# Attention rows by halves of the head: values, key sums and division in column tiles of 32, weights rounded in pieces of 768

## Chip, core and metric

One core of one Trainium2 chip. The metric is device time in microseconds (us) from the first to the last instruction of an execution, with what lies around it; lower is better. All times are of single executions, or medians over several.

The engines: PE multiplies matrices (a matmul has a stationary operand, loaded ahead, and a moving one; the trace lists the loads as PEld), DVE and POOL work on tensors element by element, ACT applies functions and copies, and SP issues the DMAs here, in the order of the program. On chip, a tensor has up to 128 partitions and a row of elements in each. PE writes into eight banks of an accumulator memory (PSUM).

## What is computed

```python
def rmsnorm(x, g):
    return x / np.sqrt(np.mean(x * x, axis=-1, keepdims=True) + 1e-06) * g

# q, k, v: (8, 12, 448, 64); w_in: (768, 2048); w_out: (2048, 768)
q_n, k_n = rmsnorm(q, g_q), rmsnorm(k, g_k)
scores = 1.0 / np.sqrt(64) * np.matmul(q_n, k_n.transpose(0, 1, 3, 2))
attn = np.exp(scores - np.max(scores, axis=-1, keepdims=True))
attn = attn / (np.sum(attn, axis=-1, keepdims=True) + 1e-09)
x = np.matmul(attn, v).transpose(0, 2, 1, 3).reshape(8 * 448, 768)
h = x @ w_in
out = (h - np.tanh(h)) @ w_out
```

The two weights arrive as float64, as pairs of 32-bit words, and are rounded to float32 on the chip. All else is float32.

## The kernel before

**Steps.** Attention is cut into 48 steps: 8 batches by 6 pairs of heads. A step s loads k, q and v of two heads (`load`), takes the mean squares of rows (`norm`: POOL squares into `sq`, L325; DVE sums, L326; POOL raises to the power -0.5, L330), scales q (`norm_q`, L336), turns k and q on PE (`turn`, L348 and L352), multiplies keys by queries (`scores`, L372; row tiles of 64), and takes exponentials on ACT (L377), with no maximum subtracted, as the gains bound the scores. So keys lie in the partitions of `p`, in four chunks of 112, and queries in its rows.

**Sums and values.** `values` (L398) multiplies v by `p`: for each chunk and head a matmul with 64 stationary columns and 448 moving ones; head 0 fills partitions 0 to 63 of a bank, head 1 the other 64. The sum over keys is a matmul with ones. From step 8 on, `add` (L389, L391) first adds the four chunks on DVE, so that one part is left for PE; the steps before have four. `totals` (L410) uses 64 columns of ones, so the sums come out repeated over the partitions as the values lie, and `divide` (L452) multiplies by their reciprocal (L415) in one instruction; its output is scattered with a step of four elements, since a chunk takes every fourth row. Steps 12 to 47 use `totals_by_halves` (L425): four column tiles of 32, each with one head and one half of the queries; the reciprocal has 224 elements in a row then (L430), but does not lie as the values do. So one row of each tile goes to DRAM (`rows_out`, L435) and comes back repeated over 64 partitions (`rows_in`, L443).

**MLP.** After a batch's six steps its x, 6 tiles of 128 x 448, goes through both products by a scheme with seven products in place of eight, on halves of rows and columns. `divide` makes the sums of tiles that it needs for steps 3 to 5 of a batch (`tt`, L465 to L468, on DVE in batch 0, on POOL later). `hidden` makes 28 products for a batch, 12 matmul records each, and evicts each from its bank in `use` (L562 to L583); `project` makes 21 (L620 to L634); batch 0 uses `project_first` (L659) with plain products. All run as a stream of matmuls that the slots advance by a planned number of nanoseconds (`run`).

**Slots.** Instructions of each engine run in the order of the program, which is written out by hand. `first_slot` runs for s from -3 to 5: no MLP yet. `slot` runs for steps 6 to 11, with batch 0's MLP between, `late_slot` for steps 12 to 47. In a `first_slot` the order is: `scores` of step s+1 (first half), `turn` of s+2, loads of s+4, `norm` of s+3, weights, `totals` of s, `scores` (second half), `divide(values)` of s, `norm_q` of s+3, weights. PSUM banks go round: 5 for scores and the like, 3 for products.

**Weights.** Rounding a piece takes two ACT instructions (L71, L72), three on DVE (L78, L79, L82) and one on POOL (L90). Before, there are 64 pieces of 128 x 384. `weight(to)` goes on to piece `to`: it issues part a of a piece, part b of the one before, part c of finished ones, and loads for as many further pieces as have room: the first 16 in nine places of the later tensor gT, then four buffers `w_raw`. `due` says at which product which piece must be done. After 8 pieces `combine_weights` (L260 to L263) makes the sums of blocks for the seven products, and `keep_weights` stores them in DRAM; `combine_w_out` (L278 to L283) does so for w_out. Batches 1 to 7 read them back through a ring of six places (`ring_load`, L311 and L313).

Of the kernel before, what the change touches and what calls it, by code (L numbers as in the profile page):

```python
# [20 lines left out]
NCH = 4  # L21
# [71 lines left out]
def bounded_path(tc, ctx, q, k, v, moe_w_in, moe_w_out, out, g_col, ident, ones, neg_half):  # L93
# [14 lines left out]

    nc = tc.nc
# [11 lines left out]
    EARLY = 16  # L121
# [60 lines left out]
    NSTAGE = CF * S // DM  # L182
# [10 lines left out]
    def weight_piece(n):  # L193

        if n < 2 * CF:
            j, f, blk = n // 8, n % 8 // 4, n % 4
            p, low, i = ((1, 0, 0), (0, 1, 0), (4, 1, 1), (2, 0, 1))[blk]
            return 2 * j + f + low * HF, i, built(j, p)[:, f]
        i, f = 1 - (n - 2 * CF) // CF, n % CF
        if i == 0:  # L200
            f = f // 2 + f % 2 * HF
        return f, i, w_out_row(f, i)

    def weight_load(n):

        f, i, _ = weight_piece(n)
        if n < EARLY:
            raw = stage[:, n % NSTAGE * DM : (n % NSTAGE + 1) * DM].rearrange("p (f w) -> p f w", w=2)
        else:
            raw = wp.tile([P, HALF, 2], I32, name="w_raw", bufs=4)  # L210
        if n < 2 * CF:
            rows = w_in_words[i * HALF : (i + 1) * HALF, f * 2 * P : (f + 1) * 2 * P]
            nc.sync.dma_start(
                out=raw.rearrange("p (c f) w -> p c (f w)", c=HC),
                in_=rows.rearrange("(c p) f -> p c f", p=P),
            )
        else:
            nc.sync.dma_start(
                out=raw.rearrange("p f w -> p (f w)"),
                in_=w_out_words[f * P : (f + 1) * P, 2 * i * HALF : 2 * (i + 1) * HALF],  # L220
            )
        raws[n] = raw
# [4 lines left out]
    def place_free(n):  # L227

        if n < EARLY:
            return n - NSTAGE < done[2]  # L230
        return n - 4 < max(done[2], EARLY)

    def weight(to):

        while done[1] < min(to, 4 * CF):
            n = done[1]
            round_weight_a(nc, raws[n], weight_piece(n)[2])
            if n:
                round_weight_b(nc, raws[n - 1], weight_piece(n - 1)[2])
            done[1] = n + 1  # L240
            finish_weights(n - 1 if n < EARLY else n)
            while done[0] < min(n + 6, 4 * CF) and place_free(done[0]):
                weight_load(done[0])
                done[0] += 1
            if kept[1] < kept[0] and n >= 8 * kept[0] + 3:
                keep_weights()
        if done[1] == 4 * CF > done[2]:
            round_weight_b(nc, raws[4 * CF - 1], weight_piece(4 * CF - 1)[2])
            finish_weights(4 * CF)

    def finish_weights(to):
        while done[2] < to:
            round_weight_c(nc, raws.pop(done[2]), weight_piece(done[2])[2])
            done[2] += 1
            if done[2] % 8 == 0 and done[2] <= 2 * CF:
                combine_weights(done[2] // 8 - 1)
# [136 lines left out]
    def values(s, av):  # L393
        v_nat = loaded.pop(("v", s))
        for c in range(NCH):
            p = probs[s, c // 2]
            for h in range(2):
                nc.tensor.matmul(  # L398
                    av[h * D : (h + 1) * D, :S], lhsT=v_nat[:, h, c, :], rhs=p[:, h, c % 2, :],
                    start=(c == 0), stop=(c == NCH - 1),  # L400
                )
        return av

    def totals(s, dn):

        t = sums.pop(s)
        parts = t if t else [probs[s, c // 2][:, :, c % 2, :] for c in range(NCH)]
        for i, p in enumerate(parts):
            for h in range(2):
                nc.tensor.matmul(  # L410
                    dn[h * D : (h + 1) * D, :S], lhsT=ones[:CP, :D], rhs=p[:, h, :],
                    start=(i == 0), stop=(i == len(parts) - 1),
                )
        rd = whole[s] = sp.tile([P, S], F32, name="rd")
        nc.vector.reciprocal(rd, dn[:, :S])  # L415

    def totals_by_halves(s, dn):

        t = sums.pop(s)
        parts = t if t else [probs[s, c // 2][:, :, c % 2, :] for c in range(NCH)]  # L420
        for i, p in enumerate(parts):
            for h in range(2):
                for n in range(2):
                    r = (2 * h + n) * BL
# [7 lines left out]
    def rows_out(s):  # L432
        rs = whole[s]
        row = whole[s] = scratch.tile([2, S], F32, name="row", bufs=2)
        nc.sync.dma_start(  # L435
            out=row.rearrange("h (n q) -> (h n) q", n=2), in_=rs.rearrange("(g i) q -> g i q", i=BL)[:, 0, :]
        )

    def rows_in(s):

        row = whole[s]
        rd = whole[s] = sp.tile([P, S], F32, name="rd")
        nc.sync.dma_start(  # L443
            out=rd,
            in_=bass.AP(tensor=row.tensor, offset=row.offset, ap=[[S, 2], [0, D], [1, S]]),
        )

    def divide(s, av):
        b, hp = steps[s]
        rd = whole.pop(s)  # L450
        x = xT[b, hp] = xp.tile([P, S], F32, name="xT")
        nc.vector.tensor_tensor(  # L452
            out=x.rearrange("r (p c) -> r c p", c=NCH), in0=av[:, :S].rearrange("r (c p) -> r c p", c=NCH),
            in1=rd.rearrange("r (c p) -> r c p", c=NCH), op=ALU.mult,
        )
# [17 lines left out]

    due = [min(EARLY + m + 1, 3 * 8) for m in range(9)]
    due += [3 * 8 + m + 1 for m in range(8)]
    due += [2 * CF + CF * (m + 1) // 11 for m in range(11)]
    assert len(due) == 7 * SETS and due[-1] == 3 * CF
# [7 lines left out]
    def products(b, layer, count, width, depth, moving, done_with):  # L485
# [8 lines left out]
        def product(j, p, bank, first):  # L494
            if b == 0:
                weight(due[7 * j + ORDER.index(p)])
                w = built(j, p).rearrange("p f (c d) -> p (f c) d", d=P)
# [3 lines left out]
            for f in range(width):  # L501
                for c in range(depth):
                    nc.tensor.matmul(  # L503
                        bank[:, f * HS : (f + 1) * HS], lhsT=w[:, f * depth + c, :], rhs=moving[p](c),
# [19 lines left out]
    def hidden(b):  # L524
# [17 lines left out]
        def done_with(j):  # L542
            up, down = slice(2 * j, 2 * j + 2), slice(HF + 2 * j, HF + 2 * j + 2)
            s1, s2, s5, u3 = part("s1"), part("s2"), part("s5"), part("u3")
# [14 lines left out]
            def use(p, bank):  # L559
# [9 lines left out]
                elif p == 7:  # L569
                    nc.vector.tensor_tensor(out=u3, in0=v, in1=s5, op=ALU.add)  # L570
                    nc.vector.tensor_tensor(out=s1, in0=v, in1=s1, op=ALU.add)

                    def rest():
                        shrink(down, high, u3, nc.gpsimd)
# [31 lines left out]
    def project(b):  # L606
# [7 lines left out]
        def done_with(j):  # L614
            y1, y2, s1, s5 = (part(n).rearrange("p f s -> p (f s)") for n in ("s2", "u3", "s1", "s5"))

            def use(p, bank):
# [3 lines left out]
                elif p == 5:  # L621
                    nc.vector.tensor_tensor(out=s5[:, low], in0=v, in1=s1[:, low], op=ALU.add)
# [4 lines left out]
                elif p == 7:  # L627
                    nc.vector.tensor_tensor(out=y2[:, high], in0=v, in1=s5[:, low], op=ALU.add)
# [12 lines left out]
    def project_first(b):  # L641
# [6 lines left out]
        for m in range(CD * CF):  # L648
# [4 lines left out]
            if k < HC:  # L653
                weight(3 * CF + CF * (m + 1) // (HC * CF))
# [48 lines left out]
    def first_slot(s):  # L703
# [8 lines left out]
        ahead = 3 * (s + 4) if s < 0 else 9 + (EARLY - 9) * (s + 1) // NP  # L712
        weight(ahead - 2)
# [4 lines left out]
        weight(ahead - 1)  # L718
# [33 lines left out]
    def late_slot(s):  # L752
        gap = gap_ns(s)
        totals_by_halves(s, sc_bank())
# [5 lines left out]
        rows_out(s)  # L760
# [3 lines left out]
        rows_in(s)  # L764
# [15 lines left out]
    for n in range(4):  # L780
        weight_load(n)
    done[0] = 4
# [235 lines left out]
def kernel(  # L1018
# [45 lines left out]
    ones = consts.tile([P, D], F32, name="ones")  # L1064
# [41 lines left out]
```

## Time and profile before

| | |
|---|---|
| median of 6 runs | 1549.32 us (1548.81 to 1550.89) |
| profiled execution, its own time | 1549.49 us |
| its span, first to last instruction | 1547.4 us |
| PE busy | 1472.9 us (95%) |
| PE weight loads | 1158.8 us (75%) |
| DVE busy | 784.8 us (51%) |
| ACT busy | 425.7 us (28%) |
| POOL busy | 619.2 us (40%) |
| mean granted PE clock | 0.982 |
| DMA | 255.2 MB, mean 165 GB/s |
| HBM | 220.6 MB read, 33.2 MB written |

In the profile L398 is line 398 of the kernel; `out<-in` gives the tiles that an instruction writes and reads, then partitions x elements of each. "Busy" is time in which an engine executes; weight loads overlap the matmuls. A number behind `<-` is idle time of the engine, with the instruction that ended it. One f32 matmul appears as two MATMUL records. The granted clock is the share of full clock that PE was given.

### The profile page before, as it was taken

How to read it: one execution, taken by the hardware profiler on the slowest of the kernel's cores; microseconds unless marked ns; L12 is line 12 of the kernel's file. 1: busy time of each engine (PE TensorE's matmuls, PEld its weight loads, DVE VectorE, ACT ScalarE, POOL GpSimd, SP SyncE). 2: the span in 40 equal slices, each digit the busy share in tenths (PEclk: the TensorE clock that was granted, in tenths of full speed). 3: DMA queues.
4: the chain of work that ended last, by engine and by line, in shares of the span. 5: the costliest groups of instructions: out<-in, count | busy, mean ns of one | idle time of the engine just before them, and what ended most of it. 6: DMA issues, size and time to landing. Idle time of an engine off the chain costs nothing.

```text
span 1547.4 us, 20449 instructions
## 1 busy us (share of the span) xinstructions
PE 1472.9 (95%) x7584; PEld 1158.8 (75%) x7584; DVE 784.8 (51%) x1110; ACT 425.7 (28%) x817; POOL 619.2 (40%) x463
## 2 busy tenths in 40 slices
PE   3999879988999999999999999999999999999997
PEld 1347654437878878878888887887887888889997
DVE  6778888864543355435544445434553454432321
ACT  4463334412221232212322222222231222210100
POOL 6655555633442333523453244432453335311310
PEclk9999989998999999999999999999999999999999
DMA  7535554496546555465555554556546555456563
GB/s 192 161 96 165 171 179 135 136 283 200 162 161 171 154 173 168 142 182 164 155 186 152 156 172 153 172 159 168 168 154 177 151 170 165 135 153 179 181 201 95
DMA packets 255049, 255.22 MB, mean 165 GB/s; under 512 B 143308, under 2 KB 203356, under 8 KB 254940
## 3 DMA queue, kind: packets, MB, share of 16 engines
q1 hardware_dynamic: 254616, 253.81, 55.2%
q8 instruction: 63, 1.03, 0.3%
q14 instruction: 46, 0.38, 0.1%
q10 hardware_dynamic: 324, 0.00, 0.0%
HBM read 220.60 MB, written 33.16 MB: 164 GB/s over the span
## 4 chain that ended last, share of the span: by engine, by line
PE 77%; DVE 13%; POOL 3%; issue 2%; DMA 2%; SPq 2%; ACT 0%; ACTq 0%; DVEq 0%; POOLq 0%
PE mm L503 56%; PE sc L372 8%; PE sc L398 8%; DVE w_out L79 2%; POOL sq L325 2%; DVE rr L326 1%; DVE w_out L82 1%; DVE rd L415 1%; POOL rr L330 1%; PE sc L425 1%; PE mm L410 1%; DVE w_out L78 1%; PE mm L398 1%; PE sc L352 1%; PE sc L348 1%
## 5 line engine op out<-in xcount | busy, mean ns | idle before, releaser
L377 ACT ACTIVATE p<-sc,rr 112x448 f32<-112x448 f32 x384 | 212.5, 638 | 487.4 <-PE sc L372 406.2
L503 PE MATMUL mm<-xT,w_f 128*128 128x224 f32 x1392 | 284.4, 359 | 14.0 <-DMA w_f<-w_in 11.0
L503 PEld LDWEIGHTS mm<-xT,w_f 128*128 128x128 f32 x1392 | 264.4, 193 | 32.7 <-issue 25.7
L503 PEld LDWEIGHTS mm<-gT,w_f 128*128 128x128 f32 x1344 | 251.3, 190 | 23.7 <-issue 14.0
L503 PE MATMUL mm<-gT,w_f 128*128 128x224 f32 x1344 | 267.8, 355 | 0.0
L503 PE MATMUL mm<-tt,w_f 128*128 128x224 f32 x1044 | 213.1, 354 | 5.3 <-DVE s L583 3.5
L503 PEld LDWEIGHTS mm<-tt,w_f 128*128 128x128 f32 x1044 | 195.6, 190 | 15.7 <-issue 8.0
L503 PE MATMUL mm<-tg,w_f 128*128 128x224 f32 x1008 | 200.4, 353 | 0.0
L503 PEld LDWEIGHTS mm<-tg,w_f 128*128 128x128 f32 x1008 | 189.5, 190 | 0.0
L372 PE MATMUL sc<-qT,kT 64*112 64x448 f32 x768 | 177.9, 568 | 11.8 <-DVE rd L415 11.2
L540 POOL TENSOR_TENSOR gT<-s,th 128x448 f32<-128x448 f32 x64 | 77.7, 1214 | 238.5 <-ACT th L539 238.5
L330 POOL TENSOR_TENSOR rr<-rr,neg_half 112x16 f32<-112x16 f32 (+1 forms) x49 | 140.0, 2857 | 51.0 <-DVE rr L329 50.0
L325 POOL TENSOR_TENSOR sq<-q_nat 112x512 f32<-112x512 f32 x48 | 50.0, 1041 | 255.5 <-DVE rr L326 247.4
L372 PEld LDWEIGHTS sc<-qT,kT 64*112 64x112 f32 x768 | 63.8, 175 | 106.3 <-issue 80.5
L398 PE MATMUL sc<-p,v_nat 112*64 112x448 f32 x672 | 135.2, 544 | 0.0
L326 DVE TENSOR_REDUCE rr<-sq 112x8 f32<-112x512 f32 x96 | 64.9, 676 | 84.0 <-POOL sq L325 83.8
L391 DVE TENSOR_TENSOR sum<-sum,p 112x896 f32<-112x896 f32 x80 | 97.5, 1219 | 13.4 <-ACT p L377 8.6
L452 DVE TENSOR_TENSOR xT<-sc,rd 128x448 f32<-128x448 f32 x42 | 40.7, 969 | 124.1 <-PE sc L398 118.5
L466 POOL TENSOR_TENSOR tt<-xT,tt 128x224 f32<-128x224 f32 x21 | 24.7, 1176 | 187.4 <-DVE xT L452 187.4
L398 PEld LDWEIGHTS sc<-p,v_nat 112*64 112x64 f32 x672 | 45.0, 136 | 71.3 <-issue 69.4
L659 PE MATMUL mm<-gT,w_out 128*128 128x448 f32 x192 | 77.1, 555 | 0.4 <-POOL w_out L90 0.4
L539 ACT ACTIVATE th<-s 128x448 f32<-128x448 f32 x64 | 37.1, 579 | 115.1 <-DVE s L583 58.7
(106 smaller groups left out, 1490.6 us busy)
## 6 DMA issues: line engine op xcount, KB each, us to landing
w_f<-w_in SPq DMA_DIRECT2D x196, 384.0 KB
w_f<-w_out SPq DMA_DIRECT2D x147, 512.0 KB
w_raw<-in_moe_w_out_dram SPq DMA_DIRECT2D x32, 384.0 KB
k_nat<-in_k_dram SPq DMA_DIRECT2D x96, 112.0 KB
q_nat<-in_q_dram SPq DMA_DIRECT2D x48, 224.0 KB
v_nat<-in_v_dram SPq DMA_DIRECT2D x48, 224.0 KB
out_dram<-th SPq DMA_DIRECT2D x192, 56.0 KB
w_in<-w_out SPq DMA_DIRECT2D x21, 384.0 KB
```

The costliest lines, as they stand in the source:

```text
L325: nc.gpsimd.tensor_tensor(out=sq, in0=rows, in1=rows, op=ALU.mult)
L326: nc.vector.reduce_sum(rr[:, "kq".index(name)], sq, axis=AX.X)
L330: nc.gpsimd.tensor_tensor(out=r, in0=r, in1=neg_half[:, : r.shape[1]], op=ALU.pow)
L372: nc.tensor.matmul(sc[:CP, :S], lhsT=kT[r, c * CP : (c + 1) * CP], rhs=qT[r, :], start=True, stop=True)
L377: nc.scalar.activation(p[:, h, i, :], tiles[h][:CP, :S], AF.Exp, scale=rr[:, 0, 2 * c + h : 2 * c + h + 1])
L391: nc.vector.tensor_tensor(out=t, in0=t, in1=part, op=ALU.add)
L398: nc.tensor.matmul(av[h * D : (h + 1) * D, :S], lhsT=v_nat[:, h, c, :], rhs=p[:, h, c % 2, :], start=(c == 0), stop=(c == NCH - 1),)
L452: nc.vector.tensor_tensor(out=x.rearrange("r (p c) -> r c p", c=NCH), in0=av[:, :S].rearrange("r (c p) -> r c p", c=NCH), in1=rd.rearrange ...
L503: nc.tensor.matmul(bank[:, f * HS : (f + 1) * HS], lhsT=w[:, f * depth + c, :], rhs=moving[p](c), start=(first and f == 0 and c == 0), sto ...
L539: nc.scalar.activation(th, h, AF.Tanh, bias=0.0, scale=1.0)
L540: eng.tensor_tensor(out=g[:, rows, cols], in0=h, in1=th, op=ALU.subtract)
L659: nc.tensor.matmul(bank[:, :S], lhsT=w_out_row(f, n // HC)[:, n % HC * P : (n % HC + 1) * P], rhs=g[:, f, :], start=(f == 0), stop=(f == C ...
```

## The change

x's tiles are ordered differently: partition m x 64 + h x 32 + r holds element m x 32 + r of head h, so that each half m of the head's 64 elements takes 64 partitions, with both heads in it. `values` makes four column tiles of 32 (m, h) for each chunk. `totals` is the former `totals_by_halves` for all steps, its tiles ordered by half n of the queries, then head. So 64 partitions with both heads stand on either side, and `divide` is four instructions (n, m) with 64 partitions x 224 each, whose reciprocals come from the partitions of n while the values come from those of m. `rows_out` and `rows_in` are gone, with both row tiles. w_in's rows are loaded in the same order: a piece takes four DMAs of 32 partitions.

Weights are rounded in 32 pieces of 128 x 768 in place of 64 of 384: both columns of a block at once, eight early ones in four places of gT, then three buffers. Part c of a piece now follows part b of it at once in the early ones too. `first_slot` spreads the pieces by a list; `due` halves its numbers. Tile `u3` is gone and its work is done in `s5`. The ones are 32 columns wide.

```diff
-    EARLY = 16
+    EARLY, PIECES = 8, 2 * CF
...
-    NSTAGE = CF * S // DM
+    NSTAGE = CF * S // (2 * DM)
...
+        if n < CF:
+            j, blk = n // 4, n % 4
             p, low, i = ((1, 0, 0), (0, 1, 0), (4, 1, 1), (2, 0, 1))[blk]
-            return 2 * j + f + low * HF, i, built(j, p)[:, f]
+            return 2 * j + low * HF, i, built(j, p)
...
-            raw = wp.tile([P, HALF, 2], I32, name="w_raw", bufs=4)
+            raw = wp.tile([P, 2 * DM], I32, name="w_raw", bufs=3)
+        if n < CF:
+            rows = w_in_words[i * HALF : (i + 1) * HALF, f * 2 * P : (f + 2) * 2 * P]
+            rows = rows.rearrange("(c h m r) f -> m h r c f", c=HC, h=2, m=2)
+            for r in range(4):
+                nc.sync.dma_start(
+                    out=raw[r * BL : (r + 1) * BL].rearrange("p (c f) -> p c f", c=HC), in_=rows[r // 2, r % 2]
+                )
...
-            finish_weights(n - 1 if n < EARLY else n)
-            while done[0] < min(n + 6, 4 * CF) and place_free(done[0]):
+            finish_weights(n)
+            while done[0] < min(n + 4, PIECES) and place_free(done[0]):
...
-            for h in range(2):
-                nc.tensor.matmul(
-                    av[h * D : (h + 1) * D, :S], lhsT=v_nat[:, h, c, :], rhs=p[:, h, c % 2, :],
-                    start=(c == 0), stop=(c == NCH - 1),
-                )
+            for m in range(2):
+                for h in range(2):
+                    r = (2 * m + h) * BL
+                    nc.tensor.matmul(
+                        av[r : r + BL, :S], lhsT=v_nat[:, h, c, m * BL : (m + 1) * BL], rhs=p[:, h, c % 2, :],
+                        start=(c == 0), stop=(c == NCH - 1),
+                    )
...
     def divide(s, av):
         b, hp = steps[s]
-        rd = whole.pop(s)
+        rs = whole.pop(s)
         x = xT[b, hp] = xp.tile([P, S], F32, name="xT")
-        nc.vector.tensor_tensor(
-            out=x.rearrange("r (p c) -> r c p", c=NCH), in0=av[:, :S].rearrange("r (c p) -> r c p", c=NCH),
-            in1=rd.rearrange("r (c p) -> r c p", c=NCH), op=ALU.mult,
-        )
+        for n in range(2):
+            for m in range(2):
+                nc.vector.tensor_tensor(
+                    out=x[m * D : (m + 1) * D].rearrange("r (p c) -> r c p", c=NCH)[:, 2 * n : 2 * n + 2],
+                    in0=av[m * D : (m + 1) * D, n * HS : (n + 1) * HS].rearrange("r (c p) -> r c p", c=2),
+                    in1=rs[n * D : (n + 1) * D].rearrange("r (c p) -> r c p", c=2), op=ALU.mult,
+                )
...
-    due = [min(EARLY + m + 1, 3 * 8) for m in range(9)]
-    due += [3 * 8 + m + 1 for m in range(8)]
-    due += [2 * CF + CF * (m + 1) // 11 for m in range(11)]
+    due = [EARLY + m // 2 + 1 for m in range(8)] + [12]
+    due += [12 + m // 2 + 1 for m in range(8)]
+    due += [CF + HF * (m + 1) // 11 for m in range(11)]
...
-        ahead = 3 * (s + 4) if s < 0 else 9 + (EARLY - 9) * (s + 1) // NP
-        weight(ahead - 2)
+        ahead = (1, 3, 4, 4, 5, 6, 6, 7, 8)[s + 3]
+        weight(ahead - 1)
...
-        totals_by_halves(s, sc_bank())
+        totals(s, sc_bank())
...
-        rows_out(s)
...
-        rows_in(s)
```

## Prediction, made before the changed kernel ran

> **What bounds the kernel now.** I read the busy shares first (PE 95% of the span), then cut the span into the stages of the program, because a mean of 95% says nothing of where the missing 5% is. The rows are: stretch, its length, busy time of PE, its weight loads, DVE, ACT, POOL (instructions), the granted clock, the DMA share, GB/s.
>
> ```profile
> 0.00:41.80 41.80, 13.51 (x48) 7.06 (x48) 26.69 (x43) 18.22 (x36) 26.49 (x24) 0.89 0.71 192
> 41.80:109.30 67.50, 65.55 (x329) 24.79 (x328) 50.29 (x68) 35.13 (x69) 38.21 (x26) 0.97 0.45 137
> 109.30:300.30 191.00, 169.68 (x687) 110.26 (x685) 164.34 (x233) 83.35 (x169) 108.12 (x88) 0.93 0.49 152
> 300.30:352.40 52.10, 41.12 (x142) 18.93 (x141) 35.58 (x42) 10.16 (x19) 22.86 (x18) 0.95 0.93 261
> 352.40:1401.00 1048.60, 1045.12 (x5657) 860.26 (x5657) 472.18 (x660) 265.24 (x499) 396.51 (x287) 1.00 0.55 164
> 1401.00:1547.40 146.40, 137.89 (x728) 137.54 (x728) 35.76 (x67) 13.64 (x27) 27.04 (x23) 0.98 0.53 160
> ```
>
> A (to 41.8) is the start: PE waits for DVE and POOL. B is the first six steps, attention alone: PE 97% busy. C is batch 0's MLP with the rounding of weights beside it: DVE 86% busy, PE short of 21 us and at a clock of 0.93. D, the second half of the first projection, is full of DMA (0.93). E, all late slots, is PE alone: 1045.1 of 1048.6. F is the last MLP. So PE work counts in B and E, DVE and POOL work in A and C, and nothing that leaves the DMA queue alone counts in D.
>
> Next come the groups that the edits replace or resemble, count and mean ns of one:
>
> ```profile
> L398 PE MATMUL sc<-p,v_nat 112*64 112x448 f32 x672 | 135.2, 544 | 0.0
> L425 PE MATMUL sc<-sum,ones 112*32 112x224 f32 x288 | 21.1, 365 | 0.0
> L430 DVE RECIPROCAL rs<-sc 128x224 f32<-128x224 f32 x36 | 56.0, 1555 | 11.5 <-PE sc L425 11.5
> L415 DVE RECIPROCAL rd<-mm 128x448 f32<-128x448 f32 x6 | 17.7, 2956 | 2.4 <-PE mm L410 2.3
> L452 DVE TENSOR_TENSOR xT<-sc,rd 128x448 f32<-128x448 f32 x42 | 40.7, 969 | 124.1 <-PE sc L398 118.5
> L564 DVE TENSOR_TENSOR s<-mm,s 128x448 f32<-128x448 f32 x32 | 20.0, 624 | 56.2 <-PE mm L503 46.0 <-ACT s L562 10.1
> L622 DVE TENSOR_TENSOR s<-mm,s 128x224 f32<-128x224 f32 x21 | 8.2, 392 | 88.4 <-PE mm L503 88.4
> L79 DVE TENSOR_SCALAR w_out<-w_out 128x384 int32<-128x384 int32 x56 | 44.0, 787 | 1.9
> L260 DVE TENSOR_TENSOR w_out<-w_out,w_out 128x768 f32<-128x768 f32 x3 | 2.9, 952 | 0.0
> ```
>
> Last, does a four-tile group run four at once? The timeline of PE, cut to the 50 ns behind 411.30, shows those that run then:
>
> ```profile
> 411.26 0.40 PE L425 MATMUL sc<-sum,ones 112*32 112x224 f32 x4
> ```
>
> All four lie in 0.40 us, each 0.377 long, so they run together. The whole group of eight begins at 411.26 and the next line, L372, at 411.78: 0.52 us. (One f32 matmul is two MATMUL records.)
>
> **Part by part.**
>
> *Values in 16 matmuls of 32 columns for 8 of 64.* The old group takes 3.16 us (426.75 to L372 at 429.90) in rounds of 0.376, two records each: eight rounds. The new one has 32 records, four to a round of the same 448 columns: again eight rounds, 3.16 us. Price 0 in all 48 steps. If only two ran together it would be 3.16 more each; the row of four is the nearest, so I take 0.
> A rule speaks against this: the Trainium skill, "TensorEngine Tiling (Array Packing)", section "Instruction Overhead", gives each matmul some 60 cycles of overhead and warns against tiling what is already small. At one column a cycle in the 0.188 us of a 224-column record that is an estimated 25 ns, and by it 16 more records cost 0.4 us a step, 19 us in all. Four records inside 0.40 us show no such sum.
>
> *Sums over keys.* Steps 0 to 7 have four parts: 16 records of 448, 3.16 us (88.07 to 91.23 in the chain). New: four groups like L425, that is eight rounds of 0.188 and the 0.15 that L425 has over its two rounds: 1.65. Saved 1.51 in 8 steps. Steps 8 to 11 have one part: 0.80 (195.66 to 196.46) becomes 0.52, saved 0.28. Steps 12 to 47 have this form already: 0. The reciprocal of 12 steps falls from 2.95 to 1.55, saved 1.40 each.
>
> *Division.* One L452 (0.97) becomes four of 64 partitions x 224. L564 to L622 gives 1.03 ns an element and 0.16 fixed; L452 has 0.346 over L564 for its scattered output, half of it 0.173. One part: 0.392 + 0.173 = 0.565; four: 2.26, so +1.29 in 48 steps. Bounds: starts overlap their predecessors by 0.09 (L570 at 417.71 for 0.62, L571 at 418.24), which gives +0.95; parts as dear as whole ones give 4 x 0.97, +2.91. I take +1.29, as rows of both sizes carry it.
> The Trainium skill, "VectorE: DVE Perf Modes", section "Two Vector instructions with no wait between them", says that an instruction whose inputs or output start in another group of 32 partitions than those before is held until all earlier ones end. The new parts change that group each time; by the rule nothing overlaps. No run so far shows it.
>
> *The row through DRAM.* L435 and L443 and 36 broadcasts of 224 KB leave SP's queue. Who waited for them: DVE, 5.0 us, once. Behind them in the queue stand loads for which PE waits only once (11.0 us, in D, ahead of the first of them). Price 0.
>
> *Rounding in pieces of 768.* Free of waits, a piece of 384 costs DVE 0.354 + 0.360 + 0.557 = 1.27. Of 768: 0.952 for the last (L260) and, with the same fixed 0.16, about 0.55 for each of the others: 2.05. That is 0.49 saved for each pair, 32 times. POOL's L90, 1.01, becomes 1.80 (the least L261 is 1.81): 0.2 saved a pair, but `sq` queued behind it waits up to 0.8 longer. Behind POOL, L79 waits (360 ns free, mean 787). In w_in each piece is now four DMAs where two pieces had two: 32 more issues of about 0.45 us on SP, ahead of k, q and v loads. They cost nothing while the queue still drains the 1.5 MB ahead of them; uncovered, the two first pieces push k_nat back by 2 us. Three buffers of 768 for four of 384 hold more bytes, so a load starts no later.
>
> **The sum by stages.**
> A: with half as many pieces, slot -1 has no rounding ahead of `norm_q`, and slot -3 none at all. L336 stood at 38.32 and took 2.45 beside POOL's L90 where 0.68 is usual; pow ended at 36.82. So turn 2 starts 38.32 + 2.45 - 36.82 - 0.68 = 3.3 earlier; I take -3.0 (0 if the SP issues eat it, -4.5 if the slots before gain too).
> B: what ends last is a loop: values, L452, the four `tt` operations (steps 3 to 5), L336, transpose, totals, scores, values. Totals give 1.51, division takes 1.29: -0.25 in steps 2, 3 and 4. Step 0 has totals at half clock (5.38): 2.7 less, and about 0.75 of the division behind it shows: -1.95. Step 1: -0.75. Step 5 ends in the MLP, which needs its x late: -1.5. Sum -5.0 (-0.5 if division costs +2.0, -9 if PE alone sets the pace).
> C: in the 126 us up to 235, DVE sets the pace: 16 pieces x 0.49, three reciprocals x 1.40, less three divisions x 1.29: -8.1. From there PE does: three totals x 0.28 and the waits for L415, of 0.82 and 2.23, shortened by 0.82 and 1.40: -3.0. POOL's longer L90 ahead of `sq` gives back up to 0.8 in half the slots, 3: in all -8 (0 to -16; the last if shorter PE waits also spare the half clock behind them, as at 131.5, where 16 matmuls took 4.98 for 3.29).
> D: SP issues without a break from 314; the same DMAs: 0 (1.5 either way).
> E and F: DVE is 1.29 later behind each division. I followed each delay to where idle time absorbs it. The nearest that PE needs then is a bank at 376.45: free 1.99 before its use, now 0.91 later. New waits begin at a delay of 2.5, and 2.9 gives 3.2 us in all. 0 (to +3).
> -3 - 5 - 8 = -16. The profiled execution took 1549.5 (span 1547.4 and 2.1 around it; the median of the runs is 1549.3): **1533.5 us**.
>
> **Rivals.**
> 1. *C keeps its pace* because buffers set it, not DVE: ACT waits 61 us there for w_raw. A ring of 3 x 768 holds little more than 4 x 384. Against: DVE is 86% busy. Then -8 alone: 1541.5.
> 2. *Coarse pieces stall PE (slower).* In batch 0's hidden layer each of 16 pieces puts twice the block ahead of an eviction on DVE and of `sq` on POOL. If each adds 1.0 to a PE wait, and every fourth drops the clock (1.7, as at 131.5), that is 23 for the 8 gained: +15 in C, +7 with A and B, 1556.5. It decides from 1.0 us a piece on. For: L566 and L415 already held PE for 4.5 and 4.1. Against: blocks come half as often, and free DVE time grows.
> 3. *Dear division*, +2.9: B loses its gain (about +2), E takes 3.2, C falls to -4: 1548 with A. No row is that dear at 224.
> 4. *Four tiles do not run together at 448*, so the change does not do what it says: 48 x 3.16 = 152, 1686 with the gains. L425 speaks against.
>
> **Chances.** Forecast 0.53 (own range 1526 to 1540), rival 1 0.24, rival 2 0.13, rival 3 0.07, rival 4 0.03. A difference of 0.2% (3 us) can be told from none here. Faster: 0.53 + 0.24 = 0.77. Same: rival 3 and the low end of 2, 0.09. Slower: 0.14. Range 1521 (A, B and C all near their lower ends) to 1549 (rivals 1 and 3 inside).
>
> **What would show it.** PE busy about 1460 (13 less: 8 x 1.51 and 4 x 0.28); DVE busy about 830 (+62 division, -17 reciprocals, -16 rounding); division groups near 0.57 us; the values group 3.16; first totals near 38.8; the DMA wait of PE still 11 us, starting near 325; late slots of 29.4 us, values group to values group, as before. Late slots longer than that, or a first ring wait later than 341, would make the prediction wrong.

## The result, and the profile after

The changed kernel takes 1553.99 us (median of 16 runs, 1550.98 to 1557.05), the kernel before 1549.24 beside it (36 runs): a ratio of 1.0028, 95% interval 1.0022 to 1.0035. It is slower by some 4.8 us where 16 less were forecast. The profiled execution has a span of 1552.2 us and a mean granted clock of 0.977 (1547.4 and 0.982 before).

The same six stages as in the prediction, at the changed kernel's own marks (stretch, length, busy time of PE, PEld, DVE, ACT and POOL, clock, DMA share, GB/s). The mark at 303.50 lies some 2.5 us ahead of the point in the work that 300.30 marked before.

```profile
0.00:41.10 41.10, 13.58 (x48) 7.05 (x48) 14.45 (x28) 16.84 (x26) 20.23 (x18) 0.90 0.84 171
41.10:117.60 76.50, 62.06 (x521) 25.58 (x520) 49.42 (x73) 35.14 (x63) 40.52 (x23) 0.88 0.57 144
117.60:303.50 185.90, 159.26 (x801) 106.37 (x800) 155.39 (x179) 78.23 (x121) 108.54 (x64) 0.93 0.51 152
303.50:359.80 56.30, 43.28 (x172) 20.42 (x170) 37.76 (x46) 10.35 (x19) 24.07 (x18) 0.89 0.91 244
359.80:1406.50 1046.70, 1044.29 (x6233) 855.49 (x6233) 528.99 (x765) 265.28 (x499) 415.94 (x287) 1.00 0.52 156
1406.50:1552.20 145.70, 137.93 (x731) 137.57 (x728) 37.06 (x70) 13.64 (x27) 27.06 (x23) 0.99 0.54 160
```

The second row is the news. Attention's first six steps (B) have 3.5 us less PE work than before (62.06 for 65.55) and last 9.0 us longer (76.50 for 67.50); their clock fell from 0.97 to 0.88. The other stages moved by some 5 us or less, the late slots by 1.9 of 1048.6.

The groups that the change is about, from the page's table of groups (count, busy us, mean ns, idle time before) and the groups by form:

```profile
L434 DVE TENSOR_TENSOR xT<-sc,rs 64x224 f32<-64x224 f32 x168 | 94.1, 560 | 127.9 <-PE sc L407 123.7
L407 PE MATMUL sc<-p,v_nat 112*32 112x448 f32 x1344 | 134.8, 542 | 0.0
L426 DVE RECIPROCAL rs<-sc 128x224 f32<-128x224 f32 x42 | 65.3, 1556 | 8.3 <-PE sc L421 7.8
L79 DVE TENSOR_SCALAR w_out<-w_out 128x768 int32<-128x768 int32 x28 | 27.2, 970 | 1.0
L269 DVE TENSOR_TENSOR w_out<-w_out,w_out 128x768 f32<-128x768 f32 x3 | 7.4, 2480 | 0.1
```

Part by part the change does what was forecast: a quarter of the division takes 0.560 us (0.565 forecast), 1344 records of values take the 135 us that 672 did, so four run together, and the reciprocal takes 1.56. Two rows take longer than they need: L79, 0.56 when undisturbed, has a mean of 0.97, and L269, a plain addition in `combine_weights`, 2.48 where its neighbour L267 takes 0.95. Neither is new by itself: before, L79 took 0.79 for 0.36, and L269's counterpart L262 took 0.96 in the first group, where attention is alone, and about 1.65 in the three later ones. What is new is that the first group, in B, is held too.

PE's waits in the whole run (in total, times, longest):

```profile
PE sc L359 <- DVE n L343: 29.2, 6, 7.0
PE mm L486 <- DMA w_f<-w_in: 13.0, 1, 13.0
PE sc L379 <- DVE rs L426: 9.1, 2, 5.8
```

The transposes of `n` wait 29.2 us for DVE, 11.0 of it in B; before, B had 1.9 us of that wait. The longest, 7.0 us, comes at the head of slot 3, ahead of the transposes of the `n` that DVE makes at the end of slot 2 (start, duration, instruction, idle time before it); the totals behind it then run at a clock of 0.54:

```profile
80.09 0.98 PE L359 MATMUL sc<-ident,n 112*128 112x112 f32 x4 [7.04 <-DVE n L343]
81.00 3.09 PE L421 MATMUL mm<-p,ones 112*32 112x224 f32 x32
```

This is what DVE does up to that `n`, and then POOL (start, duration, instruction, idle time before it):

```profile
64.73 0.96 DVE L82 SCALAR_TENSOR_TENSOR w_out<-gT,w_out 128x768 int32<-128x768 int32 x1
65.60 0.95 DVE L267 TENSOR_TENSOR w_out<-w_out,w_out 128x768 f32<-128x768 f32 x1
66.59 2.49 DVE L269 TENSOR_TENSOR w_out<-w_out,w_out 128x768 f32<-128x768 f32 x1
69.18 2.41 DVE L270 TENSOR_TENSOR w_out<-w_out,w_out 128x768 f32<-128x768 f32 x1
72.52 0.69 DVE L333 TENSOR_REDUCE rr<-sq 112x8 f32<-112x512 f32 x1 [0.93 <-POOL sq L332]
74.36 0.69 DVE L333 TENSOR_REDUCE rr<-sq 112x8 f32<-112x512 f32 x1 [1.15 <-POOL sq L332]
...
75.29 1.56 DVE L426 RECIPROCAL rs<-mm 128x224 f32<-128x224 f32 x1
76.95 2.27 DVE L434 TENSOR_TENSOR xT<-mm,rs 64x224 f32<-64x224 f32 x4
79.25 0.69 DVE L343 TENSOR_TENSOR n<-q_nat,rr 112x512 f32<-112x512 f32 x1
```

```profile
65.76 2.50 POOL L90 TENSOR_TENSOR w_out<-w_out,gT 128x768 int32<-128x768 int32 x1 [6.78 <-DVE w_out L82]
68.22 2.55 POOL L268 TENSOR_TENSOR w_out<-w_out,w_out 128x768 f32<-128x768 f32 x1
70.72 1.76 POOL L332 TENSOR_TENSOR sq<-k_nat 112x512 f32<-112x512 f32 x1
```

POOL's L90 and L268 stand ahead of the squares, so the squares begin at 70.72 though POOL had been idle for 6.78 us before L90. DVE's L269 and L270 run beside them and end some 0.8 us after them (L90 ends at 68.26, L269 at 69.08; L268 at 70.77, L270 at 71.59), so it looks as if each was held until POOL was done and then did its work. Norm sums, reciprocal, division and `n` follow one another on DVE, and only then may PE go on. Before, POOL's parts had run first (48.41 to 51.19) and DVE's three additions later (54.87 to 57.9), at 0.95 or 0.96 each:

```profile
54.87 0.95 DVE L260 TENSOR_TENSOR w_out<-w_out,w_out 128x768 f32<-128x768 f32 x1
55.85 0.96 DVE L262 TENSOR_TENSOR w_out<-w_out,w_out 128x768 f32<-128x768 f32 x1
56.92 0.96 DVE L263 TENSOR_TENSOR w_out<-w_out,w_out 128x768 f32<-128x768 f32 x1
```

The Trainium skill, "SBUF — State Buffer", section "SBUF: two separate sides", says that a DVE instruction with two inputs in SBUF (the memory of the 128 partitions) and a POOL instruction that reads there take one pair of ports in turn, and that the later one stands still until the first has ended. These rows agree.

The cause of this order is a line of the diff that the prediction read past. `finish_weights(n - 1 if n < EARLY else n)` became `finish_weights(n)`: in B, part c of a piece (L90) and the combination now follow part b at once, ahead of the next squares, where they used to come a piece later. This delay by one piece is called the lag below.

### The profile page after: what moved, and what is told of

Read it like the earlier page. It is cut to its first block, busy times and chain, and to the rows that moved or that the text cites. A ratio compares the mean times of both kernels' runs of the same rounds, so it can differ in the third digit from the quotient of the medians.

```text
span 1552.2 us, 22055 instructions
## 1 busy us (share of the span) xinstructions
PE 1460.4 (94%) x8496; PEld 1152.5 (74%) x8496; DVE 823.1 (53%) x1158; ACT 419.5 (27%) x753; POOL 636.4 (41%) x431
## 4 chain that ended last, share of the span: by engine, by line
PE 77%; DVE 9%; POOL 5%; issue 4%; DMA 2%; SPq 1%; ACT 0%; DVEq 0%; POOLq 0%; ACTq 0%
PE mm L486 56%; PE sc L379 8%; PE sc L407 7%; PE mm L642 2%; POOL sq L332 2%; POOL rr L337 1%; DVE rr L333 1%; PE sc L421 1%; DVE w_out L79 1%; DVE xT L434 1%; PE sc L359 1%; PE sc L355 1%; DVE rs L426 1%; POOL gT L523 1%; DVE w_out L82 1%
## 5 line engine op out<-in xcount | busy, mean ns | idle before, releaser
L523 POOL TENSOR_TENSOR gT<-s,th 128x448 f32<-128x448 f32 x96 | 120.6, 1263 | 263.1 <-ACT th L522 263.1
L434 DVE TENSOR_TENSOR xT<-sc,rs 64x224 f32<-64x224 f32 x168 | 94.1, 560 | 127.9 <-PE sc L407 123.7
L407 PE MATMUL sc<-p,v_nat 112*32 112x448 f32 x1344 | 134.8, 542 | 0.0
L449 POOL TENSOR_TENSOR tt<-xT,tt 128x224 f32<-128x224 f32 x21 | 29.0, 1383 | 208.4 <-DVE xT L434 208.4
L398 DVE TENSOR_TENSOR sum<-sum,p 112x896 f32<-112x896 f32 x80 | 107.3, 1341 | 9.2 <-ACT p L384 0.9
L522 ACT ACTIVATE th<-s 128x448 f32<-128x448 f32 x96 | 55.6, 579 | 171.4 <-DVE s L562 64.7
L407 PEld LDWEIGHTS sc<-p,v_nat 112*32 112x32 f32 x1344 | 40.0, 109 | 72.7 <-issue 70.0
```

The costliest lines, as they stand in the source:

```text
L398: nc.vector.tensor_tensor(out=t, in0=t, in1=part, op=ALU.add)
L407: nc.tensor.matmul(av[r : r + BL, :S], lhsT=v_nat[:, h, c, m * BL : (m + 1) * BL], rhs=p[:, h, c % 2, :], start=(c == 0), stop=(c == NCH - 1),
L434: nc.vector.tensor_tensor(out=x[m * D : (m + 1) * D].rearrange("r (p c) -> r c p", c=NCH)[:, 2 * n : 2 * n + 2], in0=av[m * D : (m + 1) * ...
L522: nc.scalar.activation(th, h, AF.Tanh, bias=0.0, scale=1.0)
L523: eng.tensor_tensor(out=g[:, rows, cols], in0=h, in1=th, op=ALU.subtract)
```

## Experiments

Three theories. **1:** the rounding in B is to blame, by its size or by the lost lag. **2:** the four-part division is. **3:** the granted clock is: with less work PE idles, the clock falls, and the gain is given back. All runs in one table; before lay at 1548.6 to 1549.2 in every comparison. Times are medians. Marks (us from the start) are from the one execution of each that was traced, which lay within some 1.5 us of the median but for e4 (2.0 below) and e12 (2.8 above). The ring wait is PE's wait for the first rounded weights that are read back.

| kernel | first totals | first MLP product | first projection | end of the ring wait | time | ratio to before (95%) |
|---|---|---|---|---|---|---|
| before | 41.8 | 109.3 | 235.2 | 352.4 | 1549.2 | |
| changed | 41.1 | 117.6 | 242.2 | 359.8 | 1554.0 | 1.0028 (1.0022 to 1.0035) |
| e1 fine rounding | 42.5 | 114.6 | 239.9 | 359.3 | 1553.0 | 1.0026 (1.0016 to 1.0037) |
| e2 coarse alone | 39.8 | 114.1 | 240.0 | 356.3 | 1551.0 | 1.0013 (1.0004 to 1.0022) |
| e3 lag | 39.0 | 110.7 | 235.2 | 352.1 | 1546.5 | 0.9985 (0.9976 to 0.9994) |
| e4 totals first | 39.1 | 114.8 | 235.4 | 352.8 | 1549.3 | 1.0002 (0.9993 to 1.0011) |
| e5 n first | 39.9 | 112.8 | 242.6 | 359.7 | 1554.1 | 1.0036 (1.0022 to 1.0049) |
| e6 four parts | 41.7 | 121.7 | 254.7 | 373.9 | 1568.3 | 1.0121 (1.0105 to 1.0136) |
| e7 three moves | 38.8 | 118.1 | 243.4 | 362.0 | 1555.2 | 1.0038 (1.0025 to 1.0052) |
| e8 unread matmuls | 39.2 | 113.3 | 238.1 | 355.7 | 1550.4 | 1.0013 (1.0004 to 1.0022) |
| e9 lag, totals first | 39.1 | 120.1 | 241.0 | 356.5 | 1552.7 | 1.0024 (1.0015 to 1.0033) |
| e10 lag, unread matmuls | 39.0 | 109.1 | 234.0 | 349.4 | 1544.5 | 0.9974 (0.9963 to 0.9985) |
| e11 coarse alone, lag | 38.7 | 110.4 | 234.6 | 352.2 | 1546.0 | 0.9983 (0.9974 to 0.9992) |
| e12 two parts | 40.6 | 109.0 | 230.3 | 345.8 | 1538.6 | 0.9938 (0.9925 to 0.9952) |
| e13 lag, two parts | 38.8 | 105.6 | 226.5 | 341.2 | 1535.4 | 0.9914 (0.9901 to 0.9928) |
| e14 late combination | 39.5 | 115.8 | 242.5 | 358.4 | 1553.6 | 1.0036 (1.0022 to 1.0050) |

From the end of the ring wait to the end of the span all changed variants need 1191.7 to 1193.5 us and before 1195.0. Whatever tells them apart happens in the first 360 us.

**e1: rounding as before, the rest as changed.**

```diff
-    EARLY, PIECES = 8, 2 * CF
+    EARLY, PIECES = 16, 4 * CF
...
-            finish_weights(n)
+            finish_weights(n - 1 if n < EARLY else n)
```

> The changed kernel with its sums, its four-part division and its x rows, but every rounding instruction takes 384 columns again, on the kernel before's schedule and with part c one piece behind (the transfers stay at 768 KB, four for a piece of w_in). Theory 1 (the loss of 9 us in the first six steps comes from the coarse rounding and from where it stands, ahead of the squares and of n): those steps, 76.5 us in the changed kernel and 67.5 before, fall to 62 to 68, and the time to some 1541 to 1546. Theory 2 (the division in four parts, 1.29 us dearer a step, makes the loop of a step longer): they stay at 75 to 77 and the time at 1552 to 1555. Theory 3 (the totals' halved work only lets TensorE's granted clock fall, so that what they save is given back): about 68 to 71 and 1547 to 1550, with the clock still near 0.88 there.

1553.0: theory 1 alone would have it near 1543. Fine rounding with its lag shortens B from 76.5 to 72.1 us, but the first totals come 1.4 later and the stretch from the first projection to the end of the ring wait takes 1.8 more, so that little is gained. Its transfers stay large; whether they are why was not tested.

**e2: the coarse rounding in the kernel before.** The edits of the diff to the weights, none of those to attention.

> The other half by itself: the kernel before with its two-part sums and its division in one instruction, but weights rounded in pieces of 768 on the changed kernel's schedule (one transfer for a piece of w_in, sum and factor of the division share a tile to make room). Theory 1: the first six steps take 74 to 80 us and the time is 1553 to 1560, no better than the changed kernel. Theory 2: 66 to 69 us there and 1545 to 1549, since the cheap division is back. Theory 3: 66 to 69 us, clock 0.95 and over, 1545 to 1549.

1551.0, between the theories: the coarse rounding as the change does it costs 2 us by itself, not 8.

**e3: the lag alone restored.**

```diff
-            finish_weights(n)
+            finish_weights(n - 1 if n < EARLY else n)
```

> The changed kernel with one thing undone: while attention is alone, GpSimd's part of a rounding (and the combination of a group) comes one piece later, as in the kernel before, so that it no longer stands right behind VectorE's part and right ahead of the next squares. Theory 1, with this lag as its cause: the first six steps fall by 4 to 9 us, the time to 1545 to 1550. Theory 1, with the size of the pieces as its cause: a fall of less than 2 us. Theories 2 and 3: no change, 1552 to 1555.

1546.5, 7.5 us less than the changed kernel and faster than before, with coarse pieces: these 7.5 us are the lag's, not the size's.

**e11: the lag restored in e2.** The same line.

> The kernel before with its own sums and division, weights rounded in pieces of 768, and GpSimd's part one piece later. Without the lag this cost 2.2 us against before. Theory 1, narrowed to the lost lag (coarse pieces are cheaper in themselves, and only the instruction that stands ahead of the next squares costs): 1541 to 1546, faster than before; and, by theory 2, no slower than the changed kernel with the lag (1546.5), since here n does not stand behind a division in four parts. If coarse pieces by themselves are dear: 1549 to 1552.

1546.0, 5.0 below e2. Coarse pieces with the lag are worth 2.5 us to the old attention (1548.6 beside it), and with them the new attention is worth nothing (1546.5 in e3). In the other two pairs it costs: 3.0 us without the lag (changed and e2), 4.2 beside fine pieces (e1 and before, though e1's transfers are larger).

**e14: the combination one piece later, L90 as changed.**

```diff
-            if done[2] % 4 == 0 and done[2] <= CF:
+            if done[2] % 4 == 1 and 1 < done[2] <= CF + 1:
```

> The changed kernel with only the combination of a group's four pieces (three additions on VectorE, one on GpSimd) issued one piece later; GpSimd's part of each rounding stays where the change put it. Theory 1 in its two forms: if the combination ahead of the third step's squares is what costs (the additions took 2.4 us instead of 0.96 there and TensorE then idled 7 us), the time falls by 4 to 7 us, to 1547 to 1550. If it is GpSimd's part of every piece, ahead of the squares, it stays at 1552 to 1555.

1553.6: no gain. Slot 2 gets shorter (`n` to `n` 12.4 us for 16.3), but the next one longer (17.9 for 14.1), and L269 and L270 take 2.48 and 2.46 there. The combination costs in whichever slot it meets POOL's part, so that L90 has to move too.

**e6: the four parts of the division in the kernel before.** L452 becomes the changed kernel's two loops.

> The kernel before with nothing changed but its division, cut into the changed kernel's four parts of 64x224 (0.56 us each instead of 1.0 us for all). Sums, layout and rounding stay as before. Theory 2: the first six steps grow from 67.5 to 71 to 75 us, with VectorE's n as what TensorE waits for, and the time to 1552 to 1557. Theories 1 and 3: no change there, 1548 to 1550.

1568.3, far beyond the 1557 that theory 2 allowed. A group of four takes 2.35 us, 1.35 more than L452 in the same steps (1.00), yet the first six steps end 13.8 us later (their last division at 122.5 for 108.7), 2.3 a step. Most of the rest is the clock; here are the totals (L410) in B, before and then in e6:

```profile
L410 PE MATMUL mm<-p,ones 112*64 112x448 f32 x96 | 21.6, 596 | 0.0
```

```profile
L410 PE MATMUL mm<-p,ones 112*64 112x448 f32 x96 | 26.2, 705 | 0.0
```

The same 96 records take 4.6 us more: those of the last two steps, behind waits of 2.36 and 2.37 us for `n`, take 4.92 and 6.01 us for 3.23, at a clock of 0.52 in the last.

**e8: unread work where PE waits.** In six slots, the first just ahead of B, before the transposes of `n`:

```diff
+        if 2 <= s < NP + 2:
+            for _ in range(8):
+                nc.tensor.matmul(
+                    tq[:BL, :HS], lhsT=ones[:CP, :BL], rhs=kn.rearrange("p c h d -> p (c h d)")[:, :HS], start=True, stop=True
+                )
```

> The changed kernel with eight matmuls of 32x224 added that nothing reads, in each of the first six steps just ahead of n's transposes, where TensorE waits for VectorE: some 1.6 us of work a step at full clock in a place where it idles. Theory 3 (the granted clock falls because TensorE idles, and a lower clock makes the step longer): the clock of these steps rises from 0.88 to 0.94 and over, the totals no longer take 3 us, and the time falls by 2 to 6 us, to 1548 to 1552. Theories 1 and 2 (VectorE and GpSimd are late, the clock only follows): no fall, 1553 to 1560.

1550.4: 3.6 us faster than the changed kernel, as theory 3 said, though the added matmuls took more than was expected of them: their 96 records take 19.3 us, 3.2 a step for the 1.6 expected. The clock from the first totals to the last division is 0.98.

**e10: the lag and the unread matmuls.**

> The changed kernel with the lag and the eight unread matmuls a step ahead of n's transposes. Theory 3, which the unread matmuls alone have borne out (3.6 us faster with 9 us more work): with the lag TensorE still waits 14 us in this stretch at a clock of 0.91, so that they bring 2 to 4 us again, 1542 to 1545. If the lag has taken away the same waits, they cost their own time: 1547 to 1553.

1544.5, the fastest here that leaves nothing out, and below both kernels of the change. Its stretch from 39.0 to the last division, and its totals, next to those of the changed kernel:

```profile
39.00:109.90 70.90, 70.90 (x605) 32.07 (x605) 48.97 (x75) 36.17 (x64) 38.47 (x23) 1.00 0.65 165
```

```profile
L426 PE MATMUL mm<-p,ones 112*32 112x224 f32 x192 | 10.3, 356 | 0.0
```

```profile
L421 PE MATMUL mm<-p,ones 112*32 112x224 f32 x192 | 15.8, 494 | 0.0
```

PE never idles, the clock is full, and the totals' halved work costs 10.3 us, close to the forecast's 9.9 (6 x 1.65); in the changed kernel it is 15.8.

**e12 and e13: half the division's instructions.** Two of 128x224, without and with the lag; the pairing of rows and factors is left out.

```diff
-            for m in range(2):
-                nc.vector.tensor_tensor(
-                    out=x[m * D : (m + 1) * D].rearrange("r (p c) -> r c p", c=NCH)[:, 2 * n : 2 * n + 2],
...
+            nc.vector.tensor_tensor(
+                out=x.rearrange("r (p c) -> r c p", c=NCH)[:, 2 * n : 2 * n + 2],
```

> The changed kernel with the division in two instructions of 128x224 instead of four of 64x224; the rows of the numerators are then multiplied with the factors of other rows, so that what is left out is the right pairing of factor and row. Some 1.1 us less on VectorE a step. Theory 2 (the price of the four parts stands behind the values and ahead of n in every one of the first twelve steps, as the 19.4 us that the parts alone cost the kernel before suggest): the first projection starts 8 to 14 us sooner than at 242.2, and the time is 1540 to 1546. Theory 1 (the lost lag is the whole cause, the attention's parts cancel): a gain of 0 to 3 us, 1551 to 1554.

> The same division in two instructions (same pairing left out), together with GpSimd's part of the rounding one piece later. If the lag and the division are two separate losses, their gains add up: 1532 to 1539, which is where the forecast of 1533.5 stood. If both lengthen the same wait, the lag's 1546 falls by less than 3 us.

1538.6 and 1535.4. A group of two takes 0.95 to 1.04 us in e12's first twelve steps, some 1.3 less than one of four. Without the lag this is worth 15.4 us, with it 11.1. The lag is worth 7.5 beside four parts and 3.2 beside two. So both are losses, and they overlap in part.

**e4, e5, e7, e9: other orders of the same work on DVE.** e4 moves `totals` and the reciprocal ahead of `norm`, beside the MLP too; e5 moves `norm_q(s + 3)` between `values` and `divide`; e7 is e4 and e5 with the lag, e9 is e4 with the lag.

> The changed kernel with the totals and their reciprocal issued ahead of the squares and norm sums of the step three later, so that the reciprocal, and the division behind it, no longer wait on VectorE behind sums that wait for GpSimd. Theory 1 says that n (behind the squares) ends the wait of TensorE, not the division: a fall of 0 to 3 us in the first six steps, 1550 to 1554. Theory 2 says that the division is what is late: a fall of 5 to 9 us, 1545 to 1549. Theory 3: no change, 1552 to 1555.

> The changed kernel with one move: in the first six steps VectorE normalises q (n) of the step three later ahead of the four-part division instead of behind it. Theory 2 in a new form (the dearer division is harmless by itself, but n stands behind it on VectorE and TensorE's transposes stand behind n, so each step's chain is longer by the 1.29 us that four parts cost): the stretch from the first totals to the MLP's first product falls from 76.5 to 69 to 73 us, the time to 1547 to 1551. Theory 1 (order and size of the rounding alone): no change, 1552 to 1555, since the rounding still stands ahead of n. Theory 3 (the clock takes back what the totals save): no change or a fall below 2 us.

> Three moves together in the changed kernel: GpSimd's part of the rounding one piece later (7.5 us by itself), totals and reciprocal ahead of the norm sums (4.7 us by itself), and n ahead of the division. If the three take away different waits, their gains add to 14 or more and the time is 1537 to 1542, below the kernel before by 7 to 12 us; if they take away one and the same wait (theory 1 alone), it stays at 1545 to 1548.

> The changed kernel with GpSimd's part of the rounding one piece later (7.5 us by itself) and totals with their reciprocal ahead of the norm sums (4.7 us by itself), n left behind the division. If both only shorten one wait, TensorE's for n, the time is 1545 to 1548, that of the lag alone. If they shorten different stages (the lag the start and the first six steps, the early totals also the steps beside batch 0's MLP, where they brought the first projection forward by 6.8 us while the first six steps ended only 2.8 us sooner), their gains add up: 1540 to 1544. Moving n ahead of the division, the third move, would then be what cost the three together 9 us or more.

e4 gained 4.7 us. Beside batch 0's MLP (first MLP product to first projection) its trace has 120.6 us for 124.6, ahead of it 2.8 less. e5 gained nothing: the MLP could begin earlier (112.8), but then the division was last, ending at 119.8 (119.0 in the changed kernel), so it seems that not `n`'s place behind it costs, but the time that DVE needs for both. e7 and e9 were slower than e3: early totals, worth 4.7 without the lag, cost 6.2 with it. In e9 the reciprocal pushes the norm sums and so POOL's power and its L90 back, and L90 then meets DVE's `n` and L79 in slot 2:

```profile
74.46 1.85 POOL L90 TENSOR_TENSOR w_out<-w_out,gT 128x768 int32<-128x768 int32 x1
```

```profile
75.42 1.43 DVE L343 TENSOR_TENSOR n<-q_nat,rr 112x512 f32<-112x512 f32 x1
76.78 0.55 DVE L78 TENSOR_SCALAR w_out<-w_out 128x768 f32<-128x768 f32 x1
77.36 2.08 DVE L79 TENSOR_SCALAR w_out<-w_out 128x768 int32<-128x768 int32 x1
```

L343 takes 0.69 and L79 0.56 when nothing holds them. But e3 has such a meeting in slot 2 as well (L343 2.15, L79 1.28), and e9 one more, a slot earlier (1.93 and 1.28). So the meetings can be only a part of e9's loss, and the rest is open.

## Why the prediction was wrong

Stage by stage, cut where the same work begins: first totals, first MLP product, second half of the first projection (291.1 before and 293.7 after; the prediction's own mark in it, 300.3, lies 16 records later), end of the ring wait:

| stage | forecast | measured |
|---|---|---|
| A | -3.0 | -0.7 |
| B | -5.0 | +9.0 |
| C, to the projection's second half | -8 | -5.7 |
| D | 0 | +4.8 |
| E and F | 0 | -2.6 |

**B failed, and the step in it that failed is the loop.** The prediction let B end by "a loop: values, L452, the four `tt` operations (steps 3 to 5), L336, transpose, totals, scores, values" and put nothing of the rounding into it, nor any lower clock but that of step 0. Three things were left out:

- *The lost lag.* "`sq` queued behind it waits up to 0.8 longer" was counted, and only in C. In B `sq` waited for L90 and L268, 5 us in slot 2, and DVE's additions with it. Restoring the lag shortens B from 76.5 to 71.7 us and the time by 7.5 (e3). Rival 2 had the mechanism, a coarse piece ahead of `sq`, but put it into batch 0's hidden layer at 1.0 us a piece, and took its drop of the clock for rare.
- *Coarse pieces even with the lag.* e11, with the old attention, has a B of 71.7 (110.4 - 38.7) where the old rounding has 67.5. These 4.2 us are more than A gained by having fewer pieces in its slots (-3.1). Before, 9 of the 16 early pieces were begun ahead of slot 0, now 4 of the 8, and the first combination has moved from the end of slot 0 to that of slot 1 or 2; presumably this is where they lie, which no run tried by itself.
- *The clock.* The prediction called B bound by PE and took 1.51 us off the totals in every step. With DVE's chain as the loop, less PE work means a longer wait, and behind it half a clock: four of the six groups of totals took 2.9 to 3.2 us and not 1.72 (the first was at half clock before as well, and forecast so; three are new). e8 and e10 show its worth: 3.6 and 2.0 us, with unread work in place of the waits.

*The division* was sized rightly (2.27 to 2.37 a group for 2.26), and with the lag old and new attention take the same time (e11, e3). The forecast for B set its +1.29 on DVE against the totals' -1.51 on PE. On DVE alone the reciprocal's -1.40 stands against it, which the forecast for B did not count, and which fits e11 and e3 as well; these runs cannot tell the two balances apart. Up to the first projection, which nine steps precede, adding 1.35 a step to the old kernel's DVE cost 19.5 us (e6), 1.6 for one; taking 1.3 a step from the changed one gained 11.9 (e12), about one for one. Rival 3 asked what happens if the instruction is dearer; it was not, but in e6's place each us of it cost more than one.

*What is left.* Lag and unread work together bring 9.5 of the 20.5 us between forecast and result. e10 still lies 11.0 above the forecast: in its trace B takes 70.1 us where 62.5 were forecast, and C with D gain 2.7 of 8. No run here brings these back without leaving something out (e13 does not pair rows and factors).

**A** was right for coarse pieces with the lag: first totals at 38.7 to 39.1 in e3, e7, e9, e10, e11 and e13, 38.8 forecast. Coarse pieces without it have them between 39.1 and 41.1, so the changed kernel's profile lies at the late end, and not only by the lag.

**C and D** must be taken together. Up to the first projection C gained 1.3 us of 8: DVE's busy time there fell only from 108.55 to 104.92, and its norm sums wait 13.0 us for `sq` where they waited 10.6. The rounding's own three lines fell from 55.0 to 41.7 us there, more than the forecast's 16 x 0.49, and the reciprocals from 8.9 to 4.7. But the division rose from 2.9 to 8.3, and `n`, the sums of chunks and the combinations took 6.4 us more together (`n` has a mean of 1.37 for 0.81, the addition L269 2.48 for L262's 1.66). For these the sum had no term. The half of the projection behind it gained 4.4.

D then took 4.8 back: it is no stretch of fixed length. Ahead of it nothing was saved a pair: the last pieces came every 3.86 us (L90 at 299.90 and 303.76), where two of 384 had taken 3.91 (295.65 to 299.56), as L79 took 2.06 there and not about 0.55. SP's first store waits for DVE behind the last piece; it came at 303.91 for 300.01, 1.3 us later counted from the second half's begin. From there to the ring's first load SP needed 51.1 us (to 354.98) for 47.8 (to 347.78). The rows of D show some 13.6 MB moved at 261 GB/s before and 13.7 MB at 244 after. Why about the same bytes went slower is open.

**E and F** held, as the delays had been followed one by one: slots of 29.4 us, no new wait. The 2.6 us gained there were not forecast; every variant has 1.5 to 3.3 of them, e2 and e6 too, which share no edit, so the one profile of before may simply be long there.

Of what would show it: PE busy 1460.4 (1460 forecast), DVE 823.1 (830) and the groups were right; the first totals (41.1 for 38.8) and the first ring wait were not: the wait began at 346.8, where later than 341 was to mean wrong, and lasted 13.0 us for 11. So the instructions that were replaced were priced well, and the sum failed on where they stand and on what they hold up. One aside was miscounted: by its own scale, 224 columns in 0.188 us, the 60 cycles cited there come to an estimated 50 ns and not 25. The values group took 3.21 us for 3.23 before, so neither shows.

## What to carry to other kernels

Before pricing an instruction, write out the loop of every engine around it, not only that of the busiest: PE was 97% busy in B, and yet a loop of DVE and POOL lay so close behind it that savings on PE went into waiting, while 1 us on DVE cost up to 1.7 (e6's 2.3 a step for 1.35). A lag in a hand-written order is part of the price of what it delays: read each index in a diff (`n - 1` to `n`) as a move, and look at what is queued behind it. And where PE must wait for two or three us again and again, a little unread work in the gap can be faster than the gap.

## What the runs showed of the hardware

The clock can fall after waits of about 2 us. In B of the changed kernel, e3 and e12, PE's waits ahead of the totals were at most 1.72 us before the groups that took 1.72, and 2.35 us or more before those that took 2.8 to 3.2; the granted clock was 0.51 in the last of these groups of the changed kernel and 1.00 in the second. Between these there is no sharp edge: 1.77 us in e8 came before 2.35, 1.91 in e9 before 2.94 and 2.18 in e1 before 2.87, but 1.89 in e9 and 2.37 in e4 before 1.72, and 2.18 in e6 was without a loss. The Trainium skill, "TensorE: Matmul & The Clock Gate", section "HAM oscillation — how this bites in real kernels", gives as the rule no idle gaps over about 3.4 us; here waits of 2.35 us were enough, if not every time, and the measurement decides.

Four DVE instructions whose partitions change follow one another without any overlap: groups of 2.27 to 2.36 us, at 0.56 each. e12's two of 128x224, whose partitions do not change, do overlap: 0.95 to 1.04 the group, at 0.57 to 0.60 each. The Trainium skill's rule on two Vector instructions with no wait between them, which the prediction cited with no run to show it, agrees.

One POOL instruction makes a DVE instruction beside it 0.7 to 1.5 us longer (L269 2.49 for 0.96, L79 2.08 for 0.56, L343 1.43 for 0.69), up to 2.7 times its own time.
